# Splitting the output projection of a recurrent block's last tokens: part at once, part behind the segment and in the next K projection

## The chip, the cores and the metric

The kernel runs on one core of a Trainium2 chip. The metric is the device time of one execution in microseconds (us), median of several executions. The profile is taken by the hardware profiler on one execution of a run. Its terms: PE is TensorE's matmul, PEld its weight load, DVE VectorE, ACT ScalarE, POOL GpSimd; L752 is line 752 of the kernel; "issue" as the releaser of a wait means that the engine waited for nothing that the profile shows. The busy times of PE and PEld are modelled, and the halved-stream run below suggests that they hold some waiting too (18.8 us busy in a first segment there, 21.3 in the kernel before, for the same instructions).

## The reference, cut to what matters

The program computes two independent things. Part A, a long convolution, takes the first 600 us and is not touched. Part B is a recurrent attention: 2048 tokens in 64 segments of 32, each with 8 memory tokens which are the output of the segment before.

```python
for s in range(n_seg):                                   # 64
    h = concat([mem, x[:, 32*s : 32*s+32]])              # 40 rows, 1024 wide
    q, k, v = h @ Wq, h @ Wk, h @ Wv                     # 32 heads of 128
    p = softmax(mask(q @ k.T * scale))
    o = einsum('bhte,hed->btd', p @ v, Wo)               # output projection over 32 heads
    mem = o[:, :8]                                       # needed by the next segment
    outs.append(o[:, 8:])
```

The four weights are 8 MB each in bf16.

## The kernel before

The weights are cut into 64 chunks of 512 KB. 43 stay resident in SBUF (`Wearly`, `Wlate`); 21, every third or so, are streamed from HBM (`WS`) anew for each segment through a ring of six places (`wring`). When TensorE is done with a streamed chunk, its place is refilled.

The kernel keeps 32 rows for the tensor engine: the 8 memory rows and the segment's first 24 tokens. The last 8 tokens of a segment influence no later segment, so their output projection can wait. Their attention outputs are gathered for a block of four segments (`OTB`, 4 x 8 = 32 rows for each head; `OT` holds the other rows' outputs) and projected in the block's fourth segment. I call this projection the *tail*. In the kernel before, it runs inside the fourth segment's own output projection:

```python
def out_proj(hps, OT):
    for hp in hps:                        # 16 chunks of two heads; 6 of them streamed
        ch = (3, hp, 0)
        w = weight(ch)
        for hh in range(2):
            h = 2 * hp + hh
            g, c, i = h // 16, (h % 16) // 4, h % 4
            lhs = [(OT[:, c, i, :], 0)]
            if j == NB - 1:                                   # the block's fourth segment
                lhs.append((OTB[:, c, 4 * g + i, :], 256))    # the tail
            for src, o in lhs:
                for dq in range(4):       # four column groups of the array side by side
                    nc.tensor.matmul(yacc[32*dq:32*dq+32, o:o+256], lhsT=src,
                                     rhs=w[:, hh*1024 + dq*256 : hh*1024 + (dq+1)*256], ...,
                                     tile_position=(0, 32*dq))
        done(ch)                          # a streamed chunk's place in the ring is refilled
# ... a segment, in TensorE's order (attention and transposes left out):
k0 = Proj(0, 0).run().evac()              # K, first half: 8 chunks, one group of 4 matmuls of 512 each
q0 = Proj(1, 0).run().evac()              # then Q, K, Q, V, V in the same way
# ...
yacc = ps_acc.tile([128, 512], F32, tag="acc", name="yacc")
out_proj(range(0, 5), OT0)
attend(1, PT1, V1, OTp)
# ...
out_proj(range(5, 8), OT0); out_proj(range(8, 16), OT1)
Y = one.tile([128, 256], BF, tag="Y", name="Y")
nc.scalar.copy(Y[:], yacc[:, 0:256])
if s + 1 < n_seg:
    fill_mem(pend[s + 1][0], Y)           # transposes (y_tp) and a copy into rec: the next segment's memory rows
# ... Y goes to HBM; in the fourth segment YB = yacc[:, 256:512] as well
```

`Proj` and `yacc` share a PSUM pool of two buffers.

Of the kernel before, what the change touches and what calls it, by code (L numbers as in the profile page):

```python
# [9 lines left out]
BF = mybir.dt.bfloat16  # L10
F32 = mybir.dt.float32
# [381 lines left out]
def b_kernel(ctx: ExitStack, tc, x, mem0, Wq, Wk, Wv, Wo, outb, n_seg):  # L393
    nc = tc.nc
    SEG = 32
    NX = 24
    NB = 4
# [16 lines left out]
    streamed = set()  # L414
# [36 lines left out]
    res = {}  # L451
# [38 lines left out]
    with ExitStack() as c0:  # L490
# [42 lines left out]
        for m in (0, 1):  # L533
            for g in range(2):
                ws = group(m, g)
                stage = st.tile([128, n_seg, 16, 8], BF, tag="stage", name="stage")
                for hl in range(16):
                    ps = ps0.tile([128, 512], F32, tag="ps0", name="kb_ps")
                    for kc in range(8):
                        nc.tensor.matmul(ps[:], lhsT=ws[kc][:, hl * 128:(hl + 1) * 128],  # L540
                                         rhs=XBT[:, kc].rearrange("p s t -> p (s t)"),
                                         start=(kc == 0), stop=(kc == 7))
                    evac(stage[:, :, hl, :], ps[:].rearrange("p (s t) -> p s t", t=8))
                o = 256 * (m + 1) + 128 * g
                nc.sync.dma_start(REC[:, :, o:o + 128], stage[:].rearrange("p s h t -> p s (h t)"))
        for g in range(2):
            ws = group(2, g)
            for tb in range(4):
                vst = st.tile([128, 4, 512], BF, tag="vst", name="vst")
                for c in range(4):  # L550
                    ps = ps0.tile([128, 512], F32, tag="ps0", name="vb_ps")
                    for kc in range(8):
                        nc.tensor.matmul(ps[:], lhsT=XBT[:, kc, 16 * tb:16 * tb + 16, :].rearrange("p s t -> p (s t)"),  # L553
                                         rhs=ws[kc][:, c * 512:(c + 1) * 512], start=(kc == 0), stop=(kc == 7))
# [13 lines left out]
    one = ctx.enter_context(tc.tile_pool(name="b_one", bufs=1))  # L568
    two = ctx.enter_context(tc.tile_pool(name="b_two", bufs=2))
    ps_acc = ctx.enter_context(tc.tile_pool(name="b_ps_acc", bufs=2, space=PSUM))  # L570
# [15 lines left out]
    def weight(ch):  # L586
        if ch in res:
            return res[ch]
        assert uses[used[0]] == ch
        return loaded[used[0]]  # L590

    def done(ch):
        if ch in streamed:
            loaded[used[0]] = None
            used[0] += 1
            fetch()
# [21 lines left out]
    with tc.manual_schedule():  # L618
# [6 lines left out]
            nc.scalar.dma_start(Y0[32 * dq + NX:32 * dq + SEG, :], mem0[:, dq * 256:(dq + 1) * 256])  # L625
        fill_mem(pend[0][0], Y0)

        OTB = None
        for s in range(n_seg):
            b, j = s // NB, s % NB  # L630
            hT, KBs, QBs = pend.pop(s)
# [16 lines left out]
            class Proj:  # L648


                def __init__(self, m, g):
                    self.m, self.g, self.kc = m, g, 0
                    self.acc = ps_acc.tile([128, 512], F32, tag="acc", name="acc")

                def run(self, n=8):
                    for kc in range(self.kc, self.kc + n):
                        ch = (self.m, kc, self.g)
                        w = weight(ch)
                        for c in range(4):
                            nc.tensor.matmul(self.acc[32 * c:32 * c + 32, :], lhsT=hT[:, kc, :],  # L660
                                             rhs=w[:, c * 512:(c + 1) * 512],
                                             start=(kc == 0), stop=(kc == 7), tile_position=(0, 32 * c))
                        done(ch)
                    self.kc += n
                    return self
# [30 lines left out]
            def softmax_b(S):  # L696
                ssum = two.tile([128, 5], F32, tag="ssum", name="ssum")
                nc.vector.tensor_reduce(out=ssum[:], in_=S, op=ALU.add, axis=AX.X)
                nc.vector.reciprocal(ssum[:], ssum[:])
                nc.vector.tensor_tensor(out=P_pad[:, :, 0:32], in0=S[:, :, 0:32],  # L700
                                        in1=ssum[:].unsqueeze(2).to_broadcast([128, 5, 32]), op=ALU.mult)
                own = P_pad[:].rearrange("p b k -> p (b k)")[:, 32:320].rearrange("p (i w) -> p i w", w=72)
                nc.vector.tensor_tensor(out=own[:, 0:4, 0:8], in0=S[:, 0:4, 32:40],
                                        in1=ssum[:, 0:4].unsqueeze(2).to_broadcast([128, 4, 8]), op=ALU.mult)
                nc.vector.scalar_tensor_tensor(
                    out=P_pad[:, 4, 32:64].rearrange("p (i t) -> p i t", i=4),
                    in0=S[:, 4:5, 32:40].to_broadcast([128, 4, 8]), scalar=ssum[:, 4:5],
                    in1=rowhead[:].unsqueeze(2).to_broadcast([128, 4, 8]), op0=ALU.mult, op1=ALU.mult)
                PT = one.tile([128, 2, 4, 40], BF, tag="PT", name="PT")
                for kb in range(2):  # L710
                    ks = slice(32 * kb, 32 * kb + 32)
                    nc.vector.transpose(out=PT[:, kb, :, 0:32], in_=P_pad[:, 0:4, ks])
                    nc.vector.transpose(out=PT[:, kb, :, 32:40], in_=P_pad[:, 4, ks])
                return PT

            def attend(g, PT, V, OTp):
                for i in range(4):
                    idx = 4 * g + i
                    cv = slice(i * 128, i * 128 + 128)
                    for c in range(4):  # L720
                        nc.tensor.matmul(OTp[:, c, idx * 40:idx * 40 + 40], lhsT=V[32 * c:32 * c + 32, cv],
                                         rhs=PT[32 * c:32 * c + 32, 0, i, :], start=True, stop=False,
                                         tile_position=(32 * c, 0))
                    for c in range(4):
                        nc.tensor.matmul(OTp[:, c, idx * 40:idx * 40 + 40], lhsT=VBs[32 * c:32 * c + 32, g, :],  # L725
                                         rhs=PT[32 * c:32 * c + 32, 1, i, :], start=False, stop=True,
                                         tile_position=(32 * c, 0))

            def o_view(g):
                return OTp[:, :, 160 * g:160 * g + 160].rearrange("p c (i q) -> p c i q", i=4)  # L730

            def evac_o(g):
                OT = one.tile([128, 4, 4, 32], BF, tag="rotA" if g else "rotB", name="OT")
                nc.scalar.copy(OT[:], o_view(g)[:, :, :, 0:32])  # L734
                return OT

            def evac_ob(g):
                nc.vector.tensor_copy(OTB[:, :, 4 * g:4 * g + 4, 8 * j:8 * j + 8], o_view(g)[:, :, :, 32:40])  # L738

            def out_proj(hps, OT):  # L740
                for hp in hps:
                    ch = (3, hp, 0)
                    w = weight(ch)
                    for hh in range(2):
                        h = 2 * hp + hh
                        g, c, i = h // 16, (h % 16) // 4, h % 4
                        lhs = [(OT[:, c, i, :], 0)]
                        if j == NB - 1:
                            lhs.append((OTB[:, c, 4 * g + i, :], 256))
                        for src, o in lhs:  # L750
                            for dq in range(4):
                                nc.tensor.matmul(yacc[32 * dq:32 * dq + 32, o:o + 256], lhsT=src,  # L752
                                                 rhs=w[:, hh * 1024 + dq * 256:hh * 1024 + (dq + 1) * 256],
                                                 start=(h == 0 and o == 0), stop=(h == 31 and o == 0),
                                                 skip_group_check=(o > 0), tile_position=(0, 32 * dq))
                    done(ch)

            if j == 0:
                OTB = one.tile([128, 4, 8, 32], BF, tag="OTB", name="OTB")
            Sp = ps_s.tile([128, 2, 5, 40], F32, tag="S", name="S")  # L760
            OTp = ps_o.tile([128, 4, 512], F32, tag="OTp", name="OTp")
            k0 = Proj(0, 0).run().evac()
            q0 = Proj(1, 0).run().evac()
            KT0 = keys(0)
            last_queries(0)
# [19 lines left out]
            pv1 = Proj(2, 1).run(4)  # L785
            attend(0, PT0, V0, OTp)
            OT0 = evac_o(0)
            PT1 = softmax_b(Sp[:, 1])
            evac_ob(0)
            pv1.run(4)  # L790
# [1 line left out]
                load_x(s + 1)  # L792
            V1 = pv1.evac()
            yacc = ps_acc.tile([128, 512], F32, tag="acc", name="yacc")
            out_proj(range(0, 5), OT0)
            attend(1, PT1, V1, OTp)
            OT1 = evac_o(1)
            evac_ob(1)
            out_proj(range(5, 8), OT0)
            out_proj(range(8, 16), OT1)  # L800
            Y = one.tile([128, 256], BF, tag="Y", name="Y")
            nc.scalar.copy(Y[:], yacc[:, 0:256])  # L802
            if s + 1 < n_seg:
                fill_mem(pend[s + 1][0], Y)
            nc.gpsimd.dma_start(bass.AP(outb.tensor, outb.offset + SEG * s * 2048, [[256, 4], [2048, 32], [1, 256]]), Y[:])  # L805
            if j == NB - 1:
                YB = one.tile([128, 256], BF, tag="OTB", name="YB")
                nc.vector.tensor_copy(YB[:], yacc[:, 256:512])
                for dq in range(4):
                    nc.gpsimd.dma_start(  # L810
                        bass.AP(outb.tensor, outb.offset + (SEG * NB * b + NX) * 2048 + 256 * dq,
                                [[2048 * SEG, NB], [2048, 8], [1, 256]]), YB[32 * dq:32 * dq + 32, :])


@with_exitstack
# [65 lines left out]
```

## Time and profile before

| | us |
|---|---|
| median of the runs | 2485.4 (2483.1 to 2495.3) |
| the recurrent loop in the profiled run (after about 600 us) | 1872 |
| segments of a block, first to fourth, mean (from one copy Y<-yacc to the next) | 28.3, 28.3, 29.2, 33.1 |
| TensorE without work, releaser "issue", mean per segment: first, fourth | 0.5, 3.0 |

First the profile's page: busy time by engine, the DMA share and GB/s in 40 slices of the span, the DMA queues (packets, MB, share of 16 engines), and the chain of waits by engine.

```profile
PE 1782.3 (72%) x33598; PEld 886.9 (36%) x33620; DVE 674.8 (27%) x2203; ACT 639.9 (26%) x1143; POOL 365.5 (15%) x1019
...
DMA  8886965579999999999999999999999999999997
GB/s 286 309 280 216 361 225 143 174 249 393 399 374 393 387 379 396 373 400 376 401 377 398 372 399 360 394 368 402 360 398 374 400 366 400 368 386 385 373 389 288
...
q1 hardware_dynamic: 287064, 800.75, 84.7%
...
q8 instruction: 263, 4.31, 0.7%
...
DMA 53%; PE 31%; issue 5%; DVE 3%; POOL 1%; ACT 1%; SPq 0%; DVEq 0%; POOLq 0%; ACTq 0%
```

From slice 10 on, in the loop, DMA is 90% busy or more; the GB/s switch between some 400 and some 370. The chain of waits gives DMA more than half of the span. The queue q8 carries instructions: 263 packets, 4.31 MB, 16 KiB each.

The windows view shows a block close to the mean, a segment per line: length, busy us and instructions of each engine, granted TensorE clock, DMA share, GB/s.

```profile
core 0: us, PE busy (x) PEld busy (x) DVE busy (x) ACT busy (x) POOL busy (x), PEclk, DMA share, GB/s
928.50:957.00 28.50, 21.73 (x468) 10.50 (x468) 6.80 (x28) 6.74 (x13) 5.97 (x17) 0.94 1.01 373
957.00:985.10 28.10, 21.37 (x468) 10.44 (x468) 6.46 (x27) 6.78 (x14) 3.60 (x13) 1.00 1.03 402
985.10:1014.40 29.30, 21.26 (x468) 10.40 (x468) 6.47 (x27) 6.81 (x14) 3.59 (x13) 1.00 1.02 392
1014.40:1047.20 32.80, 25.72 (x596) 14.42 (x596) 6.46 (x27) 6.73 (x14) 3.59 (x13) 0.95 0.97 378
```

The second and third segment move 402 and 392 GB/s. The fourth has 596 matmuls where the others have 468, some 4.3 us more of TensorE busy, and only 378 GB/s; the first after it has 373. Length times GB/s of the four lines gives 45.8 MB for the block. At the second segment's 402 GB/s that is 113.9 us, and the block takes 118.7. These 5 us are DMA running below that rate around the end of the fourth segment.

The waits of the tensor engine (who waited for whom: us in total, times, longest):

```profile
engine line waited for: us in total, times, longest us
PE acc L660 <- DMA wring<-WS: 190.7, 350, 2.4
PE yacc L752 <- DMA wring<-WS: 111.6, 207, 1.9
PE yacc L752 <- issue: 64.3, 45, 3.0
```

TensorE waits 300 us for streamed chunks in all, so it has slack, about 5 us per segment. But it also waits 64 us on the output projection for nothing the profile names. The timeline (start, length, engine, line, what, and in brackets the idle time before) of a fourth segment shows what such a wait looks like:

```profile
start us, us, engine line op out<-in xcount [idle before <-releaser]
...
2350.81 0.28 PE L752 MATMUL yacc<-wring,OT 128*32 128x256 bf16 x4
...
2350.91 0.28 PE L752 MATMUL yacc<-wring,OTB 128*32 128x256 bf16 x3
2353.28 0.27 PE L752 MATMUL yacc<-wring,OTB 128*32 128x256 bf16 x1 [2.08 <-issue]
2353.28 0.10 PEld L752 LDWEIGHTS <-OT 128*32 128x32 bf16 x4 [2.37 <-issue]
```

Three of the four matmuls of a group are issued, then nothing for 2.1 us, then the fourth. The four differ only in the columns they read of a chunk that the first three use already, so no data is missing. Counted through the trace, such gaps stand a multiple of 256 TensorE instructions apart (46 of the loop's 57 gaps that are over 0.8 us and end soon after a fetch), and the DMA records have a 16 KiB packet of queue q8 that ended 1.6 us before TensorE went on here. So I read the gap as an engine out of instructions: all 263 packets of q8 are of 16 KiB, and the spacing of the gaps says that one of them holds 256 TensorE instructions, weight loads counted (263 x 256 is 67,328; the page has 67,218 matmuls and weight loads). In the loop of this trace the fetch of a block starts 3.0 us after the last block was entered (median; 80% between 1.5 and 3.8), its packet takes 1.1 us, and at a stall TensorE goes on 1.4 us after the packet's end. Blocks that stalled took 5.9 us (median; 80% between 5.4 and 6.2), and 8 of the loop's 246 blocks passed in under 5 us.

### The profile page before, as it was taken

The page shows a single profiled execution, that of the slowest core. Times are in us where ns is not written, and L with a number is a line of the kernel's source. Part 1 is how long each engine was busy: PE and PEld are TensorE (multiplying, and loading weights), DVE is VectorE, ACT ScalarE, POOL GpSimd, SP SyncE. Part 2 cuts the span into 40 slices and gives each one's busy share as a digit, 9 for nine tenths or more (in the row PEclk, how much of TensorE's full clock was granted, in tenths as well). Part 3 has the DMA queues.
Part 4 walks back from the last instruction along what each step waited for, and adds up shares of the span by engine and source line. Part 5 has one row for each costly group of instructions (what it writes and reads, how often), then busy time and mean ns, then how long its engine had stood idle before and what let it go on. Part 6 is the DMA issues. An engine that isn't in the chain of part 4 may idle for free.

```text
span 2487.5 us, 76464 instructions
## 1 busy us (share of the span) xinstructions
PE 1782.3 (72%) x33598; PEld 886.9 (36%) x33620; DVE 674.8 (27%) x2203; ACT 639.9 (26%) x1143; POOL 365.5 (15%) x1019
## 2 busy tenths in 40 slices
PE   3555279845777777777777777777777777777776
PEld 1221044322343333433343334343434343343433
DVE  5977222111222222222222222222222222222222
ACT  6965011101222222222222222222222222222221
POOL 5034000000111101111111111111111111111011
PEclk8888679878999999999999999999999999999999
DMA  8886965579999999999999999999999999999997
GB/s 286 309 280 216 361 225 143 174 249 393 399 374 393 387 379 396 373 400 376 401 377 398 372 399 360 394 368 402 360 398 374 400 366 400 368 386 385 373 389 288
DMA packets 317559, 875.09 MB, mean 352 GB/s; under 512 B 84684, under 2 KB 92908, under 8 KB 317223
## 3 DMA queue, kind: packets, MB, share of 16 engines
q1 hardware_dynamic: 287064, 800.75, 84.7%
q0 software_dynamic: 20048, 45.76, 5.3%
q10 hardware_dynamic: 10112, 23.68, 2.8%
q8 instruction: 263, 4.31, 0.7%
q14 instruction: 72, 0.59, 0.1%
HBM read 810.69 MB, written 62.39 MB: 351 GB/s over the span
## 4 chain that ended last, share of the span: by engine, by line
DMA 53%; PE 31%; issue 5%; DVE 3%; POOL 1%; ACT 1%; SPq 0%; DVEq 0%; POOLq 0%; ACTq 0%
DMA wring<-WS 47%; PE acc L660 12%; PE yacc L752 7%; PE kb_ps L540 4%; PE vb_ps L553 2%; PE qk_tp L675 1%; DMA pw<-in_B_Wv_dram 1%; DMA Wearly<-in_B_Wk_dram 1%; DMA zt<-SZ 1%; POOL Yre L342 1%; DMA Wlate<-in_B_Wv_dram 1%; DMA X_sb<-in_B_x_dram 1%; PE S L683 1%; PE S L679 1%; ACT Y L802 0%
## 5 line engine op out<-in xcount | busy, mean ns | idle before, releaser
L660 PEld LDWEIGHTS <-rec 128*32 128x32 bf16 x12288 | 326.7, 98 | 640.2 <-issue 422.0
L660 PE MATMUL acc<-wring,rec 128*32 128x512 bf16 x3840 | 394.8, 398 | 201.1 <-DMA wring<-WS 190.7
L669 ACT CAST qkv_sb<-acc 128x512 bf16<-128x512 f32 x384 | 224.7, 585 | 843.3 <-PE acc L660 796.5
L660 PE MATMUL acc<-Wearly,rec 128*32 128x512 bf16 x4608 | 378.1, 404 | 21.6 <-DVE rec L614 21.6
L660 PE MATMUL acc<-Wlate,rec 128*32 128x512 bf16 x3840 | 331.7, 386 | 0.2 <-issue 0.2
L752 PEld LDWEIGHTS <-OT 128*32 128x32 bf16 x8192 | 239.3, 99 | 247.9 <-issue 183.3
L752 PE MATMUL yacc<-Wlate,OT 128*32 128x256 bf16 x5120 | 261.4, 283 | 30.2 <-issue 29.8
L752 PE MATMUL yacc<-wring,OT 128*32 128x256 bf16 x3072 | 183.9, 284 | 127.9 <-DMA wring<-WS 111.6
L637 POOL COPY KT<-rec 128x128 bf16<-128x128 bf16 x128 | 38.7, 302 | 657.1 <-PE S L686 591.3
L805 POOL DMA_DIRECT2D out_dram<-Y x64 | 46.2, 721 | 565.1 <-ACT Y L802 556.2
L766 DVE COPY KT<-qk_tp 128x512 bf16<-128x512 bf16 x64 | 27.2, 425 | 359.2 <-PE qk_tp L675 359.2
L614 DVE COPY rec<-y_tp 128x64 bf16<-128x64 bf16 x64 | 12.3, 192 | 405.4 <-PE y_tp L613 405.4
L734 ACT CAST OT<-OTp 128x512 bf16<-128x512 f32 x128 | 74.9, 585 | 183.6 <-PE OTp L725 179.9
L691 DVE TENSOR_REDUCE mx<-S 128x5 f32<-128x200 f32 x128 | 47.2, 368 | 244.1 <-PE S L686 238.2
L802 ACT CAST Y<-yacc 128x256 bf16<-128x256 f32 x64 | 23.8, 372 | 340.6 <-PE yacc L752 340.6
L675 PE MATMUL qk_tp<-ident,qkv_sb 128*128 128x128 bf16 x1024 | 102.8, 224 | 0.0
L752 PE MATMUL yacc<-Wlate,OTB 128*32 128x256 bf16 x1280 | 91.1, 291 | 15.7 <-issue 15.7
L607 POOL DMA_DIRECT2D rec<-REC x64 | 37.0, 578 | 403.9 <-issue 272.6
L752 PEld LDWEIGHTS <-OTB 128*32 128x32 bf16 x2048 | 82.0, 103 | 29.1 <-issue 23.0
L738 DVE CAST OTB<-OTp 128x128 bf16<-128x128 f32 x128 | 34.7, 271 | 206.9 <-ACT OT L734 206.9
L675 PEld LDWEIGHTS <-qkv_sb 128*128 128x128 bf16 x1024 | 58.5, 98 | 77.1 <-issue 62.8
L540 PE MATMUL kb_ps<-XBT,Wearly 128*128 128x512 bf16 x281 | 83.0, 384 | 1.7 <-ACT XBT L507 1.2
(197 smaller groups left out, 2163.6 us busy)
## 6 DMA issues: line engine op xcount, KB each, us to landing
wring<-WS SPq DMA_DIRECT2D x1344, 512.0 KB, 7.5
rec<-REC POOLq DMA_DIRECT2D x64, 192.0 KB, 6.3
SK<-s_sb SPq DMA_DIRECT2D x16, 512.0 KB, 4.6
SU<-s_sb SPq DMA_DIRECT2D x16, 512.0 KB, 3.4
Kg<-SK ACTq DMA_DIRECT2D x32, 256.0 KB, 5.0
Ug<-SU SPq DMA_DIRECT2D x32, 256.0 KB, 5.1
REC<-stage SPq DMA_DIRECT2D x4, 2048.0 KB, 13.2
pw<-in_B_Wv_dram SPq DMA_DIRECT2D x16, 512.0 KB, 8.2
```

The source lines that it names most:

```text
L540: nc.tensor.matmul(ps[:], lhsT=ws[kc][:, hl * 128:(hl + 1) * 128], rhs=XBT[:, kc].rearrange("p s t -> p (s t)"), start=(kc == 0), stop=(kc ...
L553: nc.tensor.matmul(ps[:], lhsT=XBT[:, kc, 16 * tb:16 * tb + 16, :].rearrange("p s t -> p (s t)"), rhs=ws[kc][:, c * 512:(c + 1) * 512], st ...
L607: nc.gpsimd.dma_start(rec[:], REC[:, s, :])
L637: nc.gpsimd.tensor_copy(KT[:, :, :, 32:40], KBs[:, 128 * g:128 * g + 128].rearrange("p (c i t) -> p i c t", c=4, i=4))
L660: nc.tensor.matmul(self.acc[32 * c:32 * c + 32, :], lhsT=hT[:, kc, :], rhs=w[:, c * 512:(c + 1) * 512], start=(kc == 0), stop=(kc == 7), t ...
L669: nc.scalar.copy(sb[:], self.acc[:])
L675: nc.tensor.transpose(tp[:, i * 128:(i + 1) * 128], sb[:, i * 128:(i + 1) * 128], ident[:])
L691: nc.vector.tensor_reduce(out=mx[:], in_=S, op=ALU.max, axis=AX.X)
L734: nc.scalar.copy(OT[:], o_view(g)[:, :, :, 0:32])
L738: nc.vector.tensor_copy(OTB[:, :, 4 * g:4 * g + 4, 8 * j:8 * j + 8], o_view(g)[:, :, :, 32:40])
L752: nc.tensor.matmul(yacc[32 * dq:32 * dq + 32, o:o + 256], lhsT=src, rhs=w[:, hh * 1024 + dq * 256:hh * 1024 + (dq + 1) * 256], start=(h == ...
L805: nc.gpsimd.dma_start(bass.AP(outb.tensor, outb.offset + SEG * s * 2048, [[256, 4], [2048, 32], [1, 256]]), Y[:])
```

## The change

The intent: take the tail out of the fourth segment's critical stretch. Heads whose Wo chunk is streamed must use the chunk while it is in the ring, so their tail matmuls stay (12 heads). The 20 heads of resident chunks can come any time: 6 behind the copy of Y, 4 behind the copy into rec, 10 between the chunks of the next K projection. The tail gets its own PSUM accumulator.

```diff
+        class Tail:
+            def __init__(self, OTB, b):
+                self.left = list(range(32))
+                self.acc = ps_acc.tile([128, 512], F32, tag="acc", name="tail_acc")
+            def head(self, h, w):
+                ...
+                for dq in range(4):
+                    o = (h % 2) * 1024 + dq * 256
+                    nc.tensor.matmul(self.acc[32 * dq:32 * dq + 32, 0:256], lhsT=self.OTB[:, c, 4 * g + i, :],
+                                     rhs=w[:, o:o + 256], start=first, stop=not self.left,
+                                     tile_position=(0, 32 * dq))
+                if not self.left:
+                    self.store()
+            def run(self, n):                       # the next n heads of resident chunks
+                for h in self.left[:n]:
+                    self.head(h, res[(3, h // 2, 0)])
@@ out_proj
-                        if j == NB - 1:
-                            lhs.append((OTB[:, c, 4 * g + i, :], 256))
+                    if tail is not None and ch in streamed:
+                        tail.head(2 * hp, w)
+                        tail.head(2 * hp + 1, w)
                     done(ch)
@@ segment
-            k0 = Proj(0, 0).run().evac()
+            k0 = Proj(0, 0)
+            for _ in range(8):
+                k0.run(1)
+                if tail is not None:
+                    tail.run(3)
+            k0 = k0.evac()
+            tail = None
@@ end of segment
             nc.scalar.copy(Y[:], yacc[:, 0:256])
+            if tail is not None:
+                tail.run(6)
             if s + 1 < n_seg:
                 fill_mem(pend[s + 1][0], Y)
             ...
+            if tail is not None:
+                tail.run(4 if s + 1 < n_seg else 32)
```

(The store of YB is as before but comes after the last tail head.) The number of instructions on every engine is the same.

More of the change, by code (lines that the diff above doesn't have):

```diff
@@ L626, in b_kernel, with store @@
         fill_mem(pend[0][0], Y0)
-        OTB = None
+        class Tail:
+            def __init__(self, OTB, b):
+                self.OTB, self.b = OTB, b
+                self.left = list(range(32))
+                self.acc = ps_acc.tile([128, 512], F32, tag="acc", name="tail_acc")
+            def head(self, h, w):
+                g, c, i = h // 16, (h % 16) // 4, h % 4
+                first = len(self.left) == 32
+                self.left.remove(h)
+                for dq in range(4):
[8 more added lines that the diff above has]
+                    self.head(h, res[(3, h // 2, 0)])
+            def store(self):
+                YB = one.tile([128, 256], BF, tag="OTB", name="YB")
+                nc.vector.tensor_copy(YB[:], self.acc[:, 0:256])
+                for dq in range(4):
+                    nc.gpsimd.dma_start(
+                        bass.AP(outb.tensor, outb.offset + (SEG * NB * self.b + NX) * 2048 + 256 * dq,
+                                [[2048 * SEG, NB], [2048, 8], [1, 256]]), YB[32 * dq:32 * dq + 32, :])
+        OTB = tail = None
         for s in range(n_seg):
@@ L746, in out_proj @@
                         g, c, i = h // 16, (h % 16) // 4, h % 4
-                        lhs = [(OT[:, c, i, :], 0)]
-                        if j == NB - 1:
-                            lhs.append((OTB[:, c, 4 * g + i, :], 256))
-                        for src, o in lhs:
-                            for dq in range(4):
-                                nc.tensor.matmul(yacc[32 * dq:32 * dq + 32, o:o + 256], lhsT=src,
-                                                 rhs=w[:, hh * 1024 + dq * 256:hh * 1024 + (dq + 1) * 256],
-                                                 start=(h == 0 and o == 0), stop=(h == 31 and o == 0),
-                                                 skip_group_check=(o > 0), tile_position=(0, 32 * dq))
+                        for dq in range(4):
+                            nc.tensor.matmul(yacc[32 * dq:32 * dq + 32, 0:256], lhsT=OT[:, c, i, :],
+                                             rhs=w[:, hh * 1024 + dq * 256:hh * 1024 + (dq + 1) * 256],
+                                             start=(h == 0), stop=(h == 31), tile_position=(0, 32 * dq))
+                    if tail is not None and ch in streamed:
+                        tail.head(2 * hp, w)
+                        tail.head(2 * hp + 1, w)
                     done(ch)
-            if j == 0:
-                OTB = one.tile([128, 4, 8, 32], BF, tag="OTB", name="OTB")
             Sp = ps_s.tile([128, 2, 5, 40], F32, tag="S", name="S")
             OTp = ps_o.tile([128, 4, 512], F32, tag="OTp", name="OTp")
-            k0 = Proj(0, 0).run().evac()
+            k0 = Proj(0, 0)
[5 more added lines that the diff above has]
+            tail = None
             q0 = Proj(1, 0).run().evac()
@@ L787, in b_kernel @@
             OT0 = evac_o(0)
+            if j == 0:
+                OTB = one.tile([128, 4, 8, 32], BF, tag="OTB", name="OTB")
             PT1 = softmax_b(Sp[:, 1])
@@ L794, in b_kernel @@
             yacc = ps_acc.tile([128, 512], F32, tag="acc", name="yacc")
+            if j == NB - 1:
+                tail = Tail(OTB, b)
             out_proj(range(0, 5), OT0)
@@ L805, in b_kernel @@
             nc.gpsimd.dma_start(bass.AP(outb.tensor, outb.offset + SEG * s * 2048, [[256, 4], [2048, 32], [1, 256]]), Y[:])
-            if j == NB - 1:
-                YB = one.tile([128, 256], BF, tag="OTB", name="YB")
-                nc.vector.tensor_copy(YB[:], yacc[:, 256:512])
-                for dq in range(4):
-                    nc.gpsimd.dma_start(
-                        bass.AP(outb.tensor, outb.offset + (SEG * NB * b + NX) * 2048 + 256 * dq,
-                                [[2048 * SEG, NB], [2048, 8], [1, 256]]), YB[32 * dq:32 * dq + 32, :])
+            if tail is not None:
+                tail.run(4 if s + 1 < n_seg else 32)
 @with_exitstack
```

## The prediction

The 256 instructions are counted in the trace above, in packets of 16 KiB. The 5 to 6.2 us for a block are an estimate, about the sum of the three times measured in the trace (2 to 3.8, 1.1 and 1.4 us), and no strict limit: 8 of the loop's 246 blocks took less than 5.

> **What bounds it now.** The change sits in the recurrent loop, 64 segments from 600 us to the end. The chain of waits puts 47% of the span on the DMA of streamed weights (wring<-WS); the page shows DMA 90% or more busy there. Each segment streams 21 chunks of 512 KB. From one copy Y<-yacc to the next (trace), the segments of a block of four take 28.3, 28.2, 29.2 and 33.1 us, 118.8 per block. At the second segment's 403 GB/s, the block's 45.8 MB would take 113.7 us. So about 5 us per block, 80 us in all, is the most that can be won.
>
> **Where the fourth segment's 4 to 5 us go.** Its output projection runs 64 groups of four matmuls instead of 32 (0.11 us each: 3.5 us more), while its DMA wait shrinks only from about 5.2 to 3.2 us. And TensorE stands still for 3.0 us with releaser "issue", against 0.5 to 0.7 elsewhere. The timeline shows gaps of 1.2 and 2.4 us inside a group, 256 TensorE instructions apart. [...] in the loop a fetch starts 2 to 3.8 us after the previous block is entered, takes 1.1 us, and TensorE resumes 1.4 us later; a block can't pass in under 5 to 6.2 us. Meanwhile the ring of six is full, DMA falls from 407 to about 200 GB/s and stays near 300 for the first 8 us of the next segment, which wins nothing back.
>
> **What the change does.** No matmul or byte is added; 128 matmuls move. 48 (heads of the 6 streamed Wo chunks) stay in the output projection, where TensorE waits for those chunks anyway; 24 run behind the copy of Y (gap 0.75 us, need 0.65), 16 behind the copy into rec (gap 0.51, need 0.44), 40 (1.1 us) between the chunks of the next K projection. y_tp comes 0.2 to 0.4 us later than Y's copy allows. The second PSUM accumulator needs the V copy done; I expect no wait.
>
> **What it is worth.** Busy time and DMA slack alone would give nearly all of the 5 us. But the instructions between the output projection's start and the K projection's end stay as many and pass two to three block borders: I expect the fourth segment's issue gap to fall from 3.0 to 1.8 us and the first's to rise by 0.6. A hand model of TensorE, ring and fetch gave 1 us per block; it reproduces half of the block's loss, so I take 2.
>
> Estimate: 15.5 blocks x 2.1 us = 33 us: **2452 us**, range 2418 to 2474. Faster by over 2%: 0.22; within 2%: 0.75; slower by over 2%: 0.03.
>
> **To be seen afterwards.** Fourth segment 29.5 to 30.5 us, first 28.7 to 29.7, others as before; the issue gap on the output projection's line smaller, on the next K projection's larger; the DMA dip after the fourth segment shallower but still there; busy times unchanged.
>
> **What would make it wrong.** If fetches start sooner once the burst is thinner, or the ring never drains, the block goes to 114 us and the time to about 2415. If the interleaved heads hold up the K projection's chunks (later refills), the loss only moves one segment on and nothing is won.

## The result, and the profile after

| | before | changed |
|---|---|---|
| median, us | 2485.4 | 2459.2 (2457.0 to 2468.6) |
| ratio | | 0.989, 95% interval 0.986 to 0.993 |
| segments of a block, first to fourth, mean us (profiled run) | 28.3, 28.3, 29.2, 33.1 | 30.2, 28.4, 29.0, 29.8 |

A ratio here and below is the mean time of one kernel's fast runs over that of the other's of the same rounds, so not quite the ratio of the medians quoted. The change wins 26 us, 1.1%: within 2%, and near the predicted 2452. The same kernel timed again with the first experiments gave 2459.6 us and again 0.989.

The page of the changed kernel, the same parts:

```profile
PE 1788.2 (72%) x33620; PEld 889.7 (36%) x33620; DVE 676.8 (27%) x2203; ACT 639.8 (26%) x1143; POOL 365.4 (15%) x1019
...
DMA  8886974669999999999999999999999999999997
GB/s 286 310 281 210 366 236 120 192 211 391 399 375 400 390 399 380 397 375 386 399 387 401 387 398 386 398 369 399 379 403 382 401 383 400 374 392 379 383 386 301
...
q1 hardware_dynamic: 287064, 800.75, 85.0%
...
q8 instruction: 263, 4.31, 0.7%
...
DMA 47%; PE 24%; issue 4%; ACT 1%; DVE 0%; POOL 0%; SPq 0%; DVEq 0%; POOLq 0%; ACTq 0%
```

Busy time, bytes and instruction packets are the same; only the slices differ, and the dips, down to 360 before, now end at some 370 to 380. The windows of a block close to the mean:

```profile
1162.70:1192.70 30.00, 23.04 (x553) 13.39 (x541) 6.89 (x28) 6.77 (x14) 5.97 (x17) 1.00 0.98 371
1192.70:1221.10 28.40, 21.53 (x468) 10.22 (x468) 6.47 (x27) 6.75 (x14) 3.61 (x13) 1.00 1.03 402
1221.10:1250.00 28.90, 21.03 (x468) 10.33 (x468) 6.47 (x27) 6.81 (x14) 3.59 (x13) 1.00 1.03 402
1250.00:1280.40 30.40, 23.70 (x519) 11.92 (x523) 6.46 (x27) 6.73 (x13) 3.59 (x13) 0.94 1.01 395
```

The fourth segment has lost 2 us of TensorE busy and 2.4 us of length, the first has got 1.3 us of busy and 1.5 us of length. The waits (L780 is the output projection, L692 the projections of K, Q and V, L642 the tail):

```profile
PE acc L692 <- DMA wring<-WS: 178.7, 325, 2.3
PE yacc L780 <- DMA wring<-WS: 104.1, 199, 1.6
PE yacc L780 <- issue: 55.0, 41, 3.5
...
PE tail_acc L642 <- issue: 17.4, 11, 2.5
```

The waits for streamed chunks fell by 20 us in all. The "issue" waits of the output projection fell from 64 to 55 us, but another 17 us stand on the tail now. So the gaps were moved, not removed. The timeline of a next K projection shows one there:

```profile
1163.43 0.28 PE L613 MATMUL y_tp<-ident,Y 128*128 128x128 bf16 x2
1163.65 0.62 PE L642 MATMUL tail_acc<-Wlate,OTB 128*32 128x256 bf16 x16
1164.09 0.39 PE L692 MATMUL acc<-Wearly,rec 128*32 128x512 bf16 x4
1164.31 0.27 PE L642 MATMUL tail_acc<-Wlate,OTB 128*32 128x256 bf16 x1
1165.83 0.51 PE L642 MATMUL tail_acc<-Wlate,OTB 128*32 128x256 bf16 x11 [1.25 <-issue]
1166.07 0.49 PE L692 MATMUL acc<-Wearly,rec 128*32 128x512 bf16 x4
```

Four heads run behind the copy into rec (16 matmuls), then the K projection's first chunk, then one matmul of the next head, and then nothing for 1.25 us, again in the middle of a group. K's next chunks are resident and ready.

The trace gives the account per block, over 15 blocks (idle time of the matmul engine by what ended it, short gaps left out, so that a row adds up to a little less than its length; two runs of the changed kernel):

| mean us per block | length | PE or PEld busy | waits for DMA | for ACT, DVE | "issue" |
|---|---|---|---|---|---|
| before, fourth | 33.05 | 25.78 | 3.18 | 0.88 | 3.04 |
| before, first | 28.27 | 21.33 | 5.54 | 0.80 | 0.46 |
| changed, fourth | 29.88, 29.96 | 23.20, 23.24 | 3.23, 3.67 | 0.86, 0.82 | 2.49, 2.12 |
| changed, first | 30.23, 29.86 | 23.74, 23.68 | 4.71, 4.32 | 0.12, 0.07 | 1.58, 1.63 |

Fourth and first together are 1.2 to 1.5 us shorter: 0.7 to 0.8 less of waits for other engines (hidden behind the two copies), 0.7 to 0.8 less of waits for DMA, and 0.3 to 0.6 *more* of "issue"; the modelled busy time falls by 0.2.

### The profile page after: what moved, and what is told of

It reads as the page before. It is cut to its first block, busy times and chain, and to the rows that moved or that the text cites. A ratio compares the mean times of both kernels' runs of the same rounds, so it can differ in the third digit from the quotient of the medians.

```text
span 2466.8 us, 76501 instructions
## 1 busy us (share of the span) xinstructions
PE 1788.2 (72%) x33620; PEld 889.7 (36%) x33620; DVE 676.8 (27%) x2203; ACT 639.8 (26%) x1143; POOL 365.4 (15%) x1019
## 3 DMA queue, kind: packets, MB, share of 16 engines
q10 hardware_dynamic: 10112, 23.68, 2.8%
## 4 chain that ended last, share of the span: by engine, by line
DMA 47%; PE 24%; issue 4%; ACT 1%; DVE 0%; POOL 0%; SPq 0%; DVEq 0%; POOLq 0%; ACTq 0%
DMA wring<-WS 47%; PE acc L692 13%; PE yacc L780 5%; PE tail_acc L642 2%; PE qk_tp L707 1%; PE S L715 1%; PE S L711 1%; PE y_tp L613 0%; PE OTp L753 0%; ACT Y L840 0%; PE S L718 0%; PE OTp L757 0%; DVE rec L614 0%; DMA out_dram<-Y 0%; SPq L583 0%
## 5 line engine op out<-in xcount | busy, mean ns | idle before, releaser
L692 PEld LDWEIGHTS <-rec 128*32 128x32 bf16 x12288 | 333.2, 98 | 606.3 <-issue 404.1
L692 PE MATMUL acc<-wring,rec 128*32 128x512 bf16 x3840 | 396.9, 398 | 187.8 <-DMA wring<-WS 178.7
L692 PE MATMUL acc<-Wearly,rec 128*32 128x512 bf16 x4608 | 389.7, 408 | 17.3 <-DVE rec L614 16.5
L692 PE MATMUL acc<-Wlate,rec 128*32 128x512 bf16 x3840 | 331.0, 385 | 0.0
L780 PEld LDWEIGHTS <-OT 128*32 128x32 bf16 x8192 | 216.5, 99 | 256.5 <-issue 190.1
L780 PE MATMUL yacc<-Wlate,OT 128*32 128x256 bf16 x5120 | 234.1, 283 | 39.3 <-issue 39.0
L780 PE MATMUL yacc<-wring,OT 128*32 128x256 bf16 x3072 | 169.4, 284 | 123.9 <-DMA wring<-WS 104.1
L676 POOL COPY QBm<-rec 128x32 bf16<-128x32 bf16 x512 | 83.8, 209 | 0.0
L642 PEld LDWEIGHTS <-OTB 128*32 128x32 bf16 x2048 | 61.9, 104 | 37.0 <-issue 26.5
```

The source lines that it names most:

```text
L642: nc.tensor.matmul(self.acc[32 * dq:32 * dq + 32, 0:256], lhsT=self.OTB[:, c, 4 * g + i, :], rhs=w[:, o:o + 256], start=first, stop=not se ...
L676: nc.gpsimd.tensor_copy(q[:, :, 40 * i:40 * i + 8], QBs[:, 128 * g:128 * g + 128].rearrange("p (c i t) -> p c i t", c=4, i=4)[:, :, i, :])
L692: nc.tensor.matmul(self.acc[32 * c:32 * c + 32, :], lhsT=hT[:, kc, :], rhs=w[:, c * 512:(c + 1) * 512], start=(kc == 0), stop=(kc == 7), t ...
L780: nc.tensor.matmul(yacc[32 * dq:32 * dq + 32, 0:256], lhsT=OT[:, c, i, :], rhs=w[:, hh * 1024 + dq * 256:hh * 1024 + (dq + 1) * 256], star ...
```

## The experiments

Two questions. Why was only about a third of the possible 5 us per block won? And what made the win? Theory F: TensorE's instruction supply. A block of 256 instructions can't pass in under some 5 to 6 us while the weight stream fills DMA (in the kernel before, 8 of the loop's 246 did), and the stretch from the fourth segment's output projection to the next K projection has as many instructions as before. Rivals: D, the moved matmuls' busy time holds up the K projection; H, the win is what is hidden behind the copies; R, what counts is how early the ring's places come free.

Each ratio is to the kernel before, on the same chip in the same rounds.

### The changed kernel again

> The changed kernel as it is, timed on the same chip as the three variants below. Both theories: about 2459 us again, ratio to before 0.985 to 0.993. Theory F (instruction fetch: a block of 256 TensorE instructions can't pass in under some 5 to 6 us while the weight stream saturates DMA, and what is lost that way drains the DMA queue): fourth and first segments of a block together about 60 us, issue gaps of TensorE of about 2.5 us in the fourth and 1.6 us in the first.

2459.6 us, ratio 0.989 (0.987 to 0.992). As expected; the fourth and first segment sum to 59.8 us.

### Half the tail's instructions, same streaming time

Two heads of a chunk side by side in the array, each in two column groups with 512 columns, in place of one head in four groups with 256. In the traces the matmuls of a group overlap: a group of four of 512 columns passes every 0.21 us, while one takes 0.40 (by its modelled end).

```diff
-                for dq in range(4):
-                    o = (h % 2) * 1024 + dq * 256
-                    nc.tensor.matmul(self.acc[32 * dq:32 * dq + 32, 0:256], ..., rhs=w[:, o:o + 256], ...)
+                for hf in range(2):
+                    o = (h % 2) * 1024 + hf * 512
+                    r = 64 * (h % 2) + 32 * hf
+                    nc.tensor.matmul(self.acc[r:r + 32, :], ..., rhs=w[:, o:o + 512], ..., tile_position=(0, r))
 # store(): VectorE adds acc[0:64] and acc[64:128]; in the K projection two heads per chunk in place of three
```

> The tail's 128 matmuls of 256 columns become 64 of 512 (the two heads of a chunk side by side in the array): the same streaming time on TensorE (0.21 us per pair), half the tail's instructions (128 fewer per block of four segments), same places but for the next K projection (one pair per chunk in five chunks). Theory F: the block loses half a fetch block, so the stalls in the fourth and first segment shrink; a hand model gives 17 us less than the changed kernel, and as it has undersized such things by half, 20 to 35 us less: about 2430 us, ratio to before 0.975 to 0.985. Rival D (the moved matmuls' busy time holds up the chunks of the K projection and so the ring's refills): the busy time is the same, so the same time as the changed kernel within 5 us, ratio 0.987 to 0.992. Result is correct up to one more rounding.

2440.2 us, ratio 0.982 (0.979 to 0.985), result correct. The DMA queue of instructions shows the edit, 8 packets of 256 instructions fewer for 16 blocks with 128 fewer each:

```profile
q8 instruction: 255, 4.18, 0.7%
```

"Issue" of fourth and first together: 2.36 us, against 3.75 in the run of the changed kernel of the same rounds. F is met, D is not. One caveat: the busy time of PE and PEld, as the profile models it, also came out 0.8 us per block lower, so not all of the 1.2 us per block (19.4 us over 16 blocks) need be the gaps. The streaming time itself is the same, as intended: where no stall comes between, a group of four tail matmuls passes in 0.11 us with 256 columns and in 0.21 us with 512 (medians of the traces).

### Twice the tail's instructions, same streaming time

The other way: each 256-column matmul becomes two of 128.

```diff
+                for q in range(2):
                     for dq in range(4):
-                        o = (h % 2) * 1024 + dq * 256
+                        o = (h % 2) * 1024 + dq * 256 + 128 * q
+                        # out, rhs: 128 columns
```

> The tail's 128 matmuls of 256 columns become 256 of 128: the same streaming time, 256 more instructions per block of four segments, one fetch block more, all in the fourth segment and the first K projection. Theory F: the model gives 67 us more than the changed kernel; 50 to 110 us more, about 2510 to 2570 us, slower than before, ratio 1.01 to 1.035. Rival D: no change of busy time, within 8 us of the changed kernel (weight loads overlap matmuls), ratio 0.987 to 0.994.

2514.1 us, ratio 1.011 (1.008 to 1.014): slower than before, result correct. (The start flag stands on one half only.) What D says of weight loads can be seen in the trace of the kernel before: from 2345.5 to 2346.7 us groups of four matmuls start every 0.11 us, and groups of four weight loads, 0.11 us each, run beside them without a gap. Sixteen packets of instructions more, and the waits, L643 being the tail:

```profile
q8 instruction: 279, 4.57, 0.7%
```

```profile
PE tail_acc L643 <- issue: 45.2, 22, 3.4
PE yacc L782 <- issue: 44.6, 39, 3.5
```

"Issue" of fourth and first: 6.01 us. 256 more instructions per block cost 3.4 us per block, of which 2.3 are these gaps. (The modelled busy time rose by 1.0 us per block as well.) F is met, D is out. Here a group of four passes in 0.056 us, again the same time per column, so no cost per matmul shows outside the stalls. The paired, the changed and the split kernel have the same multiply work in the tail; with 128, 256 and 512 tail instructions per block, weight loads counted, they take 2440, 2460 and 2514 us.

### Almost no tail

Only three of the 32 heads are computed; the result is wrong.

```diff
-                self.left = list(range(32))
+                self.left = [0, 1, 29]          # head() returns at once for all others
```

> Wrong on purpose: of the tail's 32 heads only three are computed (29 left out, 116 matmuls per block fewer), all else as in the changed kernel. It tells what the tail costs at all, wherever it stands: the floor of any placing. Both theories: the four segments become nearly alike, 28.2 to 28.9 us each, block 113.5 to 115 us. By F's model 27 us below the changed kernel, doubled as above 40 to 55 us: 2405 to 2420 us, ratio 0.966 to 0.975. If the pair variant comes near this one although it keeps all of the tail's busy time, busy time isn't the cost (F); if the pair variant stays with the changed kernel and only this one is fast, it is (D).

2428.0 us, ratio 0.976 (0.973 to 0.979), less of a win than expected by 8 us at least. So 29 of the tail's 32 heads cost 59 us in the kernel before, 32 us in the changed one and 12 us in the paired one. The paired kernel keeps the tail's multiply work and pays a fifth of what the kernel before pays. The first segment still takes 29.3 us here, against 28.7 of the others; what holds it I did not examine.

### All resident heads in the segment's own turn

```diff
-                tail.run(6)
+                tail.run(32)     # all 20 heads left, before fill_mem; none for the K projection
```

> Undoes one part: no tail head goes into the next K projection; all 20 heads of resident chunks run behind the copy of Y, before the transposes (2.2 us there). The streamed heads stay as changed. Theory F: the same instructions in the same stretch, a little denser, so most of the gain over before goes: the model gives 11 us more than the changed kernel, 10 to 25 us more, 2469 to 2485 us, ratio 0.993 to 0.999. Rival D (the heads between the K projection's chunks hold up the ring's refills, as a slower K projection): faster than the changed kernel, ratio below 0.988.

2481.6 us, ratio 0.999 (0.995 to 1.002): the win is gone. (The result came out wrong, which I had not foreseen: by the program's order YB is now stored before Y, and the fourth segment's Y covers 8 of its rows. The stores' order is thus a second difference of this run.) So in this run the streamed/resident split alone won nothing; without heads past the start of the K projection there was no gain, the order of the stores aside. The account suggests how: the first segment waits 5.76 us for DMA, where the changed kernel waits 4.3 to 4.7. Run in one lump, the heads use up no wait; run among the projection's chunks, they do. That fits F's number and doesn't tell F from R.

### Heads later in the K projection

```diff
-            for _ in range(8):
+            for kc in range(8):
                 k0.run(1)
-                if tail is not None:
+                if tail is not None and kc >= 3:       # chunk 3 is the first streamed one
                     tail.run(3)
```

> The changed kernel with one thing moved: in the next K projection the ten heads run after its chunks 3 to 6 (three each, then one) instead of after chunks 0 to 3. Chunk 3 is the first streamed one, so the first free place in the ring, and with it the first refill, comes nine heads (1.0 us) earlier; matmuls, instructions and fetch blocks are the same. Theory R (what a block of four loses is the time in which the ring is full and no chunk is used up, whatever fills that time: matmuls of the tail or a fetch stall): 8 to 16 us less than the changed kernel (8 by the hand model), 2443 to 2451 us, ratio 0.983 to 0.987, the DMA dip of the first segment shallower. Theory F alone (only the number of instructions in the stretch counts): within 4 us of the changed kernel, ratio 0.988 to 0.991.

2455.0 us, ratio 0.989 (0.987 to 0.991). R asked for 0.983 to 0.987; the run is where F alone had it. In the trace the first streamed chunk is used 2.7 us after the copy of Y instead of 3.7, but the third, fourth and fifth 0.4 to 0.5 us later: the heads have only changed sides. So R in this simple form falls.

### All twenty heads in the K projection

```diff
-                    tail.run(3)          # and: kc >= 3
+                    tail.run(5)
-                tail.run(6)
+                tail.run(0)
-                tail.run(4 if s + 1 < n_seg else 32)
+                tail.run(0 if s + 1 < n_seg else 32)
```

> The changed kernel with no resident head in the segment's own turn: all twenty run in the next K projection, five each after its chunks 3 to 6. What the change hides behind the copy of Y and the copy into rec is given up, but the first refill comes earlier by all heads that stood before it (nineteen, less the 1.1 us hidden). Theory R: about as e7_late or better, 8 to 20 us less than the changed kernel, 2439 to 2451 us, ratio 0.981 to 0.987. Rival H (the gain of the change is what it hides in the two copies' gaps, 1.1 us per block, 17 us in all): most of the gain is lost, 2470 us or more, ratio 0.994 or more.

2458.6 us, ratio 0.990 (0.988 to 0.992): the same as the changed kernel, neither R's nor H's number. H is out: nothing is hidden behind the copies now (waits for ACT and DVE in the first segment are back at 0.78 us), yet nothing is lost, because "issue" fell to 0.98 and waits for DMA to 4.16 in the first segment. What one kind of gap doesn't take, another does.

### Less DMA: the stream halved

Does a fetch take long by itself (F2) or because DMA is full (F1)? Each streamed chunk loads only its first 256 KB and is read twice; wrong.

```diff
-            nc.sync.dma_start(t[:], stream_src(uses[n]))
+            nc.sync.dma_start(t[:, 0:1024], stream_src(uses[n])[:, 0:1024])
 # and the column offsets of streamed chunks taken modulo the half
```

> The kernel before, wrong on purpose: each streamed chunk loads only its first half (256 KB) and the matmuls read that half twice; instructions, their order and their times on TensorE are the same. The weight stream then needs about half of DMA. Theory F1 [...]: with few bytes queued a fetch starts about 1.1 us after the last block was entered, as the few lightly loaded fetches of the kernel before did, and a block passes in about 3.6 us; the issue gaps of the fourth segment fall from 3.0 to below 1 us, and segments take what TensorE needs: about 23.5 us, the fourth 27 (3.5 us of matmuls more), 2130 to 2200 us in all. Rival F2 (a fetch takes some 5 to 6 us whatever DMA does): the denser program stalls more, issue gaps of 3 us and more in the fourth and over 1 us in the others.

( The 1.1 us: in the trace of the kernel before, 18 of the loop's fetches start 1.0 to 1.2 us after the last block was entered, with DMA 63% busy in that time (median); where it takes over 2 us (203 times), DMA is full by the median.)

One look, state unknown: 2022.8 us, well under the range I gave, because the segments sank to 21.1 to 21.6 us and the fourth to 25.7. (For the same instructions the modelled busy time of a first segment is 18.8 us here and 21.3 in the kernel before; the granted clock was 0.945 against 0.931, so what I had taken for TensorE's need seems to have held waiting.) DMA and the waits of TensorE:

```profile
DMA  8979598447688878888878878887888888888885
...
q1 hardware_dynamic: 287064, 448.43, 68.8%
...
q8 instruction: 263, 4.31, 0.9%
```

```profile
PE acc L660 <- DMA wring<-WS: 32.3, 59, 1.8
```

The same 263 instruction packets. "Issue" in the fourth segment fell from 3.04 to 0.39 us. Over the loop, a fetch starts (median) 1.7 us after the last block was entered, against 3.0 in the kernel before; blocks that did stall took a little over 4 us (median) against 5.9 (80% between 5.4 and 6.2); all stalls that ended with a fetch sum to some 25 to 30 us against 90. In the kernel before, 8 of the loop's 246 blocks passed in under 5 us, here 111. F2 falls, and F1 holds in the main: with less of a weight stream, fetches come sooner. Only some two thirds of the excess over the 1.1 us that I expected went, though. One reason may be that DMA was not halved: q1 has as many packets as before, each half as large, and its share fell only from 84.7% to 68.8%. So bytes and packets are not told apart, nor what a fetch waits for before it starts.

> The changed kernel with the same halved stream, wrong on purpose. Theory F1: bound by TensorE, the change can win only what it hides behind the copy of Y and the copy into rec, 1.1 us per block, so 10 to 20 us less than the halved kernel before; the fourth segment's 3.5 us of tail are seen again, split between fourth and first. Rival (placing wins in itself by taking work off a bound TensorE): more than 40 us less.

One look, state unknown: 2019.0 us, 4 us less than the halved kernel before; I had expected 10 to 20. Fourth and first sum to 46.2 us against 46.8: 2.5 us less in the one, 1.9 more in the other. Four runs of the kernel before spread over 12 us, so one pair of single runs doesn't tell 4 us from 0 or from 10; the rival's 40 us are excluded. That fits a change which needs the waits for DMA, but doesn't show it.

### Pairing with the old placing

The two-by-two: the placing of the kernel before (all heads at once), with the paired tail.

```diff
-                    if tail is not None and ch in streamed:
+                    if tail is not None:
                         tail.head(2 * hp, w)
                         tail.head(2 * hp + 1, w)
 # no tail.run() behind Y; store() where the kernel before had it
```

> The placing of the kernel before (every tail head at once, inside the fourth segment's output projection, nothing behind Y or in the K projection) with the paired tail (64 matmuls of 512 columns, 128 TensorE instructions fewer per block, same busy time). With before, changed and e1_pair it makes two by two: placing and number of instructions. Theory F: most of what the kernel before loses in its fourth segment is fetch stall, so the pairing alone wins at least as much as the change of placing alone (26 us): the hand model says 30 us less than before; 25 to 40 us, 2445 to 2460 us, ratio 0.984 to 0.990, issue gap of the fourth segment from 3.0 to about 1.2 us. Theory P (the change won by giving the tail's matmul time to places where TensorE waits for DMA, and fetch is only the rest): pairing without placing wins less than 15 us, 2470 us or more, ratio above 0.994.

2454.3 us, ratio 0.988 (0.985 to 0.990), as F expected. "Issue" in the fourth segment fell to 2.17 us, not to the 1.2 I had named. That is 0.9 us per block, where the time fell by 1.8; the modelled busy time of the fourth fell by another 0.9, and how much of that is stall the records don't tell.

| median us (ratio) | 256 tail instructions | 128 tail instructions |
|---|---|---|
| all in the fourth segment | 2485 (1) | 2454 (0.988) |
| split as in the change | 2459 (0.989) | 2440 (0.982) |

Each alone wins about 1.1 to 1.2%, both together 1.8%: they win partly the same time.

### Pairing everywhere

What follows is to pair the heads in every segment's output projection. The two halves of each sum are added by the matmul that turns Y (against two stacked identities) and, for the output, by VectorE.

```diff
-                        for dq in range(4):
-                            nc.tensor.matmul(yacc[32 * dq:32 * dq + 32, 0:256], ..., rhs=w[:, hh * 1024 + dq * 256:...])
+                        for hf in range(2):
+                            r = 64 * hh + 32 * hf
+                            nc.tensor.matmul(yacc[r:r + 32, :], ..., rhs=w[:, hh * 1024 + hf * 512:...], tile_position=(0, r))
@@ fill_mem
-            nc.tensor.transpose(tp[:, half * 128:(half + 1) * 128], Y[:, half * 128:(half + 1) * 128], ident[:])
+            nc.tensor.matmul(tp[:, q * 64:(q + 1) * 64], lhsT=Y[:, q * 128:(q + 1) * 128], rhs=R2[:], start=True, stop=True)
```

> A candidate to beat both: the pairing of heads (64 matmuls of 512 columns where there were 128 of 256) in the main output projection of every segment as well as in the tail. Streaming time is the same, TensorE instructions per segment fall by 128 (of 881). The two halves of the sum are added by the matmul that turns Y (against two stacked identities) and, for the output, on VectorE. Theory F: the out projection no longer meets the fetch limit, issue gaps below 0.5 us in all segments, block 113.5 to 114.5 us as DMA alone would have it: 2405 to 2430 us, ratio 0.967 to 0.978. Rival D: no gain over the paired tail (2440 us) or a loss by the longer copy of Y (0.585 for 0.372 us, 14 us in all).

2432.3 us, ratio 0.978 (0.975 to 0.980), correct, at the slow end of what I expected: 2.2% under the kernel before and 1.1% under the changed one. The page and the waits:

```profile
GB/s 278 311 277 207 361 282 113 199 185 400 400 397 395 395 398 387 401 399 394 388 396 398 392 399 397 398 397 395 393 396 395 400 397 400 395 397 398 396 398 303
...
q8 instruction: 224, 3.67, 0.6%
```

```profile
PE acc L698 <- DMA wring<-WS: 164.4, 294, 1.8
PE yacc L787 <- DMA wring<-WS: 154.2, 273, 2.4
```

No "issue" wait of TensorE on the output projection is among the long ones any more; in fourth and first together it is 0.25 us. The GB/s no longer dip: 387 to 401 through the loop. It comes near the kernel without a tail (2428) but not under it. (The 881 instructions of my expectation are too few: a segment has 468 matmuls and as many weight loads, 936; the argument doesn't rest on it.) "Issue" in the second and third segment, 0.7 us each before, is 0.1 now, and their length is still 28.4 and 28.7 us; there the stalls had cost little, for TensorE waits more than 5 us for DMA in each.

> The paired kernel (tail and main output projection) with the tail's five pairs after chunks 3 to 7 of the K projection. Theory R and F together: there is little left to win, 0 to 10 us less than the paired kernel, 2422 to 2434 us, ratio 0.974 to 0.979; the first segment comes down from 29.4 to about 29 us.

The paired kernel with the heads moved as in the later-heads experiment (`kc >= 3`): 2431.9 us, ratio 0.979 (0.978 to 0.981), the same time. The first segment came down from 29.4 to 28.9 us, as expected, and the others rose by as much.

## Why the prediction was right, and where it was off

- *The time.* 2452 predicted, 2459 measured, in the range; 33 us of gain predicted, 26 measured. Right, but in part by luck: the hand model gave 1 us per block and was doubled by judgement, and one of its terms, the shrinking gaps, came out with the other sign (below).
- *What bounds the kernel and the ceiling of 80 us.* Borne out: no run with the whole weight stream went past the ceiling; the kernel almost without a tail wins 59 us, and the fully paired one 53.
- *A block of 256 instructions passes in no less than 5 to 6.2 us, and the change doesn't lift that.* Right with few exceptions: 8 of the loop's 246 blocks took under 5 us before and 9 after, and the stalled ones 5.9 and 6.1 us (medians). That this sets the cost is shown by the paired and the split tail, which leave the multiply work and change the count of instructions.
- *"I expect the fourth segment's issue gap to fall from 3.0 to 1.8 us and the first's to rise by 0.6."* Off. It fell to 2.1 to 2.5 and rose by 1.1. In sum the gaps did not shrink at all (3.50 before, 3.75 to 4.07 after). The forecast of 2.1 us per block took a part of the gain from here. The measured gain is 1.6 us per block (26 over 16), and by the account of the fourth and first segment it comes from 0.7 to 0.8 us of waits for ACT and DVE and 0.7 to 0.8 of waits for DMA, less the 0.3 to 0.6 by which "issue" grew.
- *The segments.* Fourth 29.5 to 30.5 expected, 29.8 and 30.0 measured. First 28.7 to 29.7 expected, 30.2 and 29.9 measured: over by 0.2 to 0.5, where "issue" was over by some 0.5.
- *The DMA dip shallower but still there.* Right. From the trace's bytes in the 28 us around the end of the fourth segment, DMA falls short of 405 GB/s by 4.8 us of transfer before, 3.3 and 2.8 after, 0.8 to 0.9 without a tail.
- *"y_tp comes 0.2 to 0.4 us later"* and the second accumulator without a wait: no wait for it is to be seen. But neither matters, since the kernel with nothing behind Y takes the same time.
- *What would make it wrong: the loss only moves one segment on.* This was half true: 1.6 to 2.0 of the fourth segment's 3.1 to 3.2 us came back in the first.

What is shown: the number of tail instructions sets most of what the tail costs; the heads' exact places in the K projection don't matter within 5 us. Shown in a single look only: a fetch starts later with the full weight stream (3.0 us after the last block was entered, against 1.7 with half its bytes). Shown by one run with a second difference: some heads of the unpaired tail must go past the start of the K projection. What is argued only: that they win by running in waits for DMA rests on the account of idle times, and on the halved stream, where TensorE waits for DMA 0.4 to 0.7 us per segment and the change wins 4 us in single runs, within their scatter. Why placings with quite different idle times (behind the copies or not, early or late) end within 5 us of each other stays open beyond that account.

## What to carry to other kernels

Count an engine's instructions, not only its busy time: if a stretch issues 256 of them in less than the time in which a block passed here (5 to 6 us, with DMA 90% busy and more), suspect that the engine runs dry; the profile showed it as an "issue" gap inside a group of matmuls, at equal distances in instructions. Fewer and wider instructions for the same work were worth as much here as moving the work elsewhere (2454 against 2459 us), and took no rescheduling. And work moved out of a bound stretch wins only as far as the place it goes to has waits to give; ask what else crosses the new place, instructions included.
